# Decode attention in an adaLN block: values in 16384-byte runs, probabilities turned on VectorE, and a loop whose order is written out

## The chip, the cores and the metric

The kernel runs on one core of one Trainium2 chip. Its time is device microseconds for one execution. The engines are PE (TensorE, matrix products), PEld (its weight loads), DVE (VectorE), ACT (ScalarE), POOL (GpSimd) and SP (SyncE, which here only issues transfers). Sixteen DMA engines move data from the memory (HBM) to the on-chip buffers (SBUF); products are written to PSUM.

## What is computed

One decode step of a transformer block for two sequences (B = 2) of one token each, all in float32. The part that matters is the attention in the middle, over the last 4096 keys of a cache:

```python
W = min(4096, max(256, Sk // 4))                       # 4096
q = (x @ wq).reshape(B, Sq, Hq, Dh)                    # 32 heads of 128
k = repeat(k_cache[:, :, Sk - W:, :], rep, axis=1)     # 8 key heads, 4 query heads on each
v = repeat(v_cache[:, :, Sk - W:, :], rep, axis=1)
scores = einsum("bhqd,bhkd->bhqk", q, k) * (Dh ** -0.5)
p = softmax(scores, axis=-1)
o = einsum("bhqk,bhkd->bhqd", p, v)
...                                                    # @ wo, residual, layer norm, SiLU feed-forward
```

Ahead of it stand a modulation (silu(c) @ w_mod), a layer norm and the query product; behind it the product with wo, a second layer norm and a feed-forward with w1 and w2.

## The kernel before

**Transfers.** All loads are issued by SP, in the order of the program: w_mod (4 pieces), wq (4), then for the 16 pairs (h, b) of key head and sequence one key tile and one value tile of 2048 KB, then wo (4), w1 (3) and w2 (5). They share a ring of 8 buffers (`ring`, tag "st", 16 KB on each partition), so a load waits until the buffer eight loads earlier has been read. `load_k` (L77) gives each partition 32 keys in a row, 16384 bytes in one run. `load_v` (L84) gives each partition four runs of 8 values, 4096 bytes each. A small load fills `x_sp` with x (L112), ahead of wq.

**The queries.** The four pieces of wq are multiplied as they land (L263), turned (L272) and spread over a mask `qbd` (L286), so that one product treats the 4 query heads of a key head in 32 columns.

**The loop** (L351) makes 17 steps; step t does the scores and the softmax of pair t and the value products of pair t-1:

- `keys` (L339): DVE turns a key tile in four pieces of 1024 columns, by blocks of 32x32 (L343), into `kT`. The pieces of pair t+1 are placed inside step t (L388, L389, L415, L416).
- PE: scores s, 16 products of 256 columns (L361), four at a time in four column groups. A float32 product is two instructions in the trace, so there are 32.
- DVE: maximum `mx` of each row (L369); PE turns it into one row, `mT` (L371); DVE takes the maximum over the groups, `mg` (L377), and writes it out as `mrow` (L383); PE makes a column of it, `bp` (L391); ACT copies it as `bias` (L393) and does the Exp with sums, `pr` (L395).
- PE turns `pr` by two products with the identity, `pT` (L408), and ACT copies that to `ptb` (L411).
- `weighted` (L296): 32 value products of 128 columns (64 instructions, L305) of the pair before, in two halves that stand on both sides of the softmax; ACT copies the result, `ob` (L314). `collect` (L317) adds it to `o_all` by one product with a selecting matrix `selh` (L319).

The program order is a priority only. A planner of the framework lays each engine's instructions in an order of its own, by what its model takes to be ready. So the value products fill gaps of PE, and things that stand behind the loop in the program (the turns `gaT`, `sbT`, `cbT` and `xT`, L420) run early.

**Behind the loop.** `on` (L452) divides by the sums, four products with `quad` (L455) turn the result, `oTn` (L458) is the operand of wo. 24 products of 512 columns (`acc_o`, L480) and 32 of 128 (`ao`, L489) follow, with a regrouping (`gather`, L462) between; then the second norm and the feed-forward (`hid` L521, `acc_yw` L554, `acc_y` L564), and the output (L577). `xT` is read at L502, `x_sp` at L536.

## Time and profile before

| | us |
|---|---|
| median of 3 runs (lowest to highest) | 241.84 (241.79 to 242.92) |
| the profiled execution itself | 242.15 |
| its span, first to last instruction | 240.0 |
| PE busy in the span | 153.6 |
| DVE busy | 102.5 |
| ACT busy | 34.9 |
| data moved | 97.82 MB, 408 GB/s over the span |
| mean granted clock of PE | 0.844 |

In the profile a line of a group names the line of the kernel, the engine and operation, output and inputs by the program's names, shapes and count; then busy time and mean duration of one in ns; then the idle time of the engine just before these instructions and what ended it. A line of the timeline begins with start and duration in us. A line of a stage begins with its start and end and its length in us, then gives busy time and number of instructions of PE, PEld, DVE, ACT and POOL, then the granted clock of PE (1.00 is full), the busy share of the DMA engines and GB/s. Products are pipelined, so a busy PE isn't a PE at its peak. SPq is SP's queue of transfers.

### The profile page before, as it was taken

The page shows a single profiled execution, that of the slowest core. Times are in us where ns is not written, and L with a number is a line of the kernel's source. Part 1 is how long each engine was busy: PE and PEld are TensorE (multiplying, and loading weights), DVE is VectorE, ACT ScalarE, POOL GpSimd, SP SyncE. Part 2 cuts the span into 40 slices and gives each one's busy share as a digit, 9 for nine tenths or more (in the row PEclk, how much of TensorE's full clock was granted, in tenths as well). Part 3 has the DMA queues.
Part 4 walks back from the last instruction along what each step waited for, and adds up shares of the span by engine and source line. Part 5 has one row for each costly group of instructions (what it writes and reads, how often), then busy time and mean ns, then how long its engine had stood idle before and what let it go on. Part 6 is the DMA issues. An engine that isn't in the chain of part 4 may idle for free.

```text
span 240.0 us, 4597 instructions
## 1 busy us (share of the span) xinstructions
PE 153.6 (64%) x2040; PEld 84.4 (35%) x2040; DVE 102.5 (43%) x179; ACT 34.9 (15%) x96; POOL 7.4 (3%) x27
## 2 busy tenths in 40 slices
PE   0293727345876596386755958478595698936854
PEld 0221101122553373253433625244363466105312
DVE  0604001684656845618548263572745721000230
ACT  2300000101411210202202022020220202020200
POOL 8000000100000000000000000000000000000000
PEclk9999775757999979959979788797978979797779
DMA  6999999999999999999999999999999999999970
GB/s 242 429 434 429 437 426 426 419 440 406 444 417 412 436 412 438 427 411 439 404 440 426 410 438 417 427 426 418 438 414 423 416 436 431 431 430 414 426 309 3
DMA packets 13755, 97.82 MB, mean 408 GB/s; under 512 B 920, under 2 KB 936, under 8 KB 9768
## 3 DMA queue, kind: packets, MB, share of 16 engines
q1 hardware_dynamic: 13736, 97.54, 97.0%
q8 instruction: 16, 0.26, 0.4%
q14 instruction: 3, 0.02, 0.0%
HBM read 97.53 MB, written 0.00 MB: 406 GB/s over the span
## 4 chain that ended last, share of the span: by engine, by line
DMA 65%; PE 17%; DVE 15%; SPq 1%; issue 1%; ACT 0%; DVEq 0%
DMA k<-in_A_k_cache_dram 38%; DMA wo<-in_A_wo_dram 12%; DMA wq<-in_A_wq_dram 12%; DVE kT L343 11%; PE s L361 7%; DMA c_ch<-in_c_dram 2%; PE hid L521 2%; PE o L305 2%; PE q L263 2%; PE acc_yw L554 1%; PE ao L489 1%; PE acc_y L564 1%; SPq L74 1%; PE mT L371 1%; DVE qbd L286 0%
## 5 line engine op out<-in xcount | busy, mean ns | idle before, releaser
L343 DVE STREAM_TRANSPOSE kT<-k 128x1024 f32<-128x1024 f32 x64 | 74.0, 1209 | 6.4 <-DMA k<-in_A_k_cache_dram 6.3
L361 PE MATMUL s<-kT,qbd 128*32 128x256 f32 x512 | 46.8, 519 | 46.6 <-DVE kT L343 46.6
L305 PE MATMUL o<-v,ptb 128*32 128x128 f32 x1024 | 45.8, 300 | 0.0
L361 PEld LDWEIGHTS s<-kT,qbd 128*32 128x32 f32 x512 | 19.4, 140 | 66.0 <-DVE kT L343 50.9
L305 PEld LDWEIGHTS o<-v,ptb 128*32 128x32 f32 x1024 | 37.0, 121 | 5.9 <-issue 3.9
L369 DVE TENSOR_REDUCE mx<-s 128x1 f32<-128x256 f32 x16 | 6.8, 424 | 46.7 <-PE s L361 46.7
L393 ACT COPY bias<-bp 128x1 f32<-128x1 f32 x16 | 2.6, 160 | 120.3 <-PE bp L391 120.3
L263 PE MATMUL q<-wq,hq_T 128*32 128x512 f32 x64 | 12.8, 940 | 10.2 <-DMA wq<-in_A_wq_dram 10.2
L395 ACT ACTIVATE pr<-s,bias 128x256 f32<-128x256 f32 x16 | 11.8, 739 | 0.5
L272 DVE STREAM_TRANSPOSE qT<-q 128x512 f32<-128x512 f32 x2 | 1.4, 716 | 20.1 <-PE q L263 20.1
L263 PEld LDWEIGHTS q<-wq,hq_T 128*32 128x32 f32 x64 | 2.3, 146 | 19.8 <-DMA wq<-in_A_wq_dram 11.0
L480 PE MATMUL acc_o<-wo,oTn 128*32 128x512 f32 x48 | 7.0, 723 | 3.3 <-DMA wo<-in_A_wo_dram 2.9
L377 DVE TENSOR_REDUCE mg<-mT 1x4 f32<-1x64 f32 x16 | 3.3, 209 | 10.9 <-PE mT L371 10.9
L371 PE MATMUL mT<-ident,mx 128*1 128x128 f32 x32 | 7.1, 308 | 1.1 <-DVE mx L369 1.1
L499 DVE STREAM_TRANSPOSE aoT<-ao 128x128 f32<-128x128 f32 x1 | 0.3, 317 | 16.7 <-PE ao L489 16.7
L408 PE MATMUL pT<-ident,pr 128*128 128x128 f32 x32 | 7.0, 301 | 0.4
L391 PEld LDWEIGHTS bp<-negscale,mrow 1*128 1x128 f32 x32 | 4.9, 190 | 5.7 <-DVE mrow L383 4.9
L391 PE MATMUL bp<-negscale,mrow 1*128 1x1 f32 x32 | 6.2, 262 | 0.8 <-DVE mrow L383 0.2
L319 PE MATMUL o_all<-ob,selh 128*32 128x128 f32 x32 | 6.5, 284 | 0.4 <-ACT ob L314 0.4
L411 ACT COPY ptb<-pT 128x256 f32<-128x256 f32 x16 | 6.0, 372 | 4.6 <-PE pT L408 4.5
L195 PE MATMUL mean_a<-mv_a,avg 128*128 128x1 f32 x2 | 0.6, 364 | 8.9 <-DVE mv_a L192 8.9
L227 PE MATMUL m_sp<-wm,scT 128*32 128x512 f32 x32 | 5.7, 796 | 0.0
(123 smaller groups left out, 90.0 us busy)
## 6 DMA issues: line engine op xcount, KB each, us to landing
k<-in_A_k_cache_dram SPq DMA_DIRECT2D x16, 2048.0 KB, 31.5
v<-in_A_v_cache_dram SPq DMA_DIRECT2D x16, 2048.0 KB, 27.0
wq<-in_A_wq_dram SPq DMA_DIRECT2D x4, 2048.0 KB
wo<-in_A_wo_dram SPq DMA_DIRECT2D x4, 2048.0 KB, 27.1
wm<-in_w_mod_dram SPq DMA_DIRECT2D x4, 1536.0 KB, 10.5
w<-in_B_w_dram SPq DMA_DIRECT2D x2, 1024.0 KB, 22.8
w<-in_B_w_dram SPq DMA_DIRECT2D x1, 1792.0 KB
w<-in_B_w_dram SPq DMA_DIRECT2D x2, 896.0 KB
```

The source lines that it names most:

```text
L263: nc.tensor.matmul(q_ps[n][32 * g : 32 * g + 32, :], hq_T[:, k, :], wv[:, n, g], start=(k == 0), stop=(k == 3),)
L305: nc.tensor.matmul(o_ps[32 * i : 32 * i + 32, :], pt[:, n % 2, o : o + 32], vt[:, i, n, :], start=(n == 0), stop=(n == 7),)
L319: nc.tensor.matmul(o_all[:, b, :], selh[:, HQ - G - G * h : 2 * HQ - G - G * h], weighted.o_sb, start=(t == 0), stop=(t == NP - 1), skip_g ...
L343: nc.vector.transpose(kT[t][:, n4].rearrange("p n j r -> p (n j r)"), kt[t][:, n4 * 1024 : (n4 + 1) * 1024],)
L361: nc.tensor.matmul(s_ps[32 * cc : 32 * cc + 32, :], qbd[h // 4][:, h % 4, b, j, :], kT[t][:, :, 2 * cc : 2 * cc + 2, j, :], start=(j == 0) ...
L369: nc.vector.tensor_reduce(mx, s_ps, axis=AX.X, op=ALU.max)
L371: nc.tensor.matmul(mT[0:1, :P], mx, ident, start=True, stop=True)
L391: nc.tensor.matmul(bp[:, 0:1], m, negscale, start=True, stop=True)
L395: nc.scalar.activation(pr.rearrange("p s k n -> p n s k"), s_ps.rearrange("p (n s k) -> p n s k", n=4, s=2), AF.Exp, bias=bias, scale=SCAL ...
L408: nc.tensor.transpose(tp[:, s * P : (s + 1) * P], pr[:, s].rearrange("p k n -> p (k n)"), ident)
L411: nc.scalar.copy(ptb[t % 2][:, :, :P], tp[:, : 2 * P].rearrange("p (s m) -> p s m", s=2))
L480: nc.tensor.matmul(acc[32 * g : 32 * g + 32, :], oTn[:, q, :], wot[q // 8][:, q % 8, :], start=(q < 4), stop=(q >= 20),)
```

## The change

- `load_v` reads values as keys are read: 32 in a row for each partition, one run of 16384 bytes.
- That fixes another order of the probabilities. DVE turns `pr` by 32x32 blocks into `xp` and multiplies it with a mask `group` of the four row groups, spreading it over `zp`; four products with `id4` on PE (`tp`, 128 columns each) sum and permute it; ACT copies 128 columns to `ptb`.
- `weighted` makes 8 products of 512 columns in place of 32 of 128. Its result has 512 columns, of which each row group holds its own block, so `collect` makes four products in place of one, `selh`, `o_all`, `lp`, `on` and `quad` have 128 rows in place of 32, and `lp` takes eight products in place of two.
- Each instruction of the loop is marked to be kept in program order on its engine (`inorder`). Step t now does the turn of pair t's keys and its scores, and in between softmax, turn and value products of pair t-1. The order is: keys 0; mT, mg, mrow; keys 1; bp, bias, Exp, xp, zp; keys 2 and 3; tp, ptb, value products; scores, mx; collect.
- `kT` is laid out by 32-column blocks first, so that a score product reads one stretch of 256 columns.
- The load of `x_sp` stands behind the loads of wo, its turn `xT` behind that. `pr`, `xp`, `zp` and `ob` have one buffer each; `ob` shares one with `qT` and the copies of `gather`.

```diff
--- before.py
+++ after.py
@@ -82,11 +82,11 @@
         return t
 
     def load_v(b, h):
-        t = stream(f"v{h}_{b}").rearrange("p (i m) -> p i m", i=4)
+        t = stream(f"v{h}_{b}")
         nc.sync.dma_start(
-            t, v_cache[b, h, SK - W :, :].rearrange("(i p n) d -> p i (n d)", i=4, p=P)
-        )
-        return t.rearrange("p i (n d) -> p i n d", d=DH)
+            t, v_cache[b, h, SK - W :, :].rearrange("(p n) d -> p (n d)", p=P)
+        )
+        return t
 
...
@@ -109,7 +109,6 @@
                 src[b, :].rearrange("(k a c) -> a k c", k=4, a=4),
             )
     wm += [load_rows("wm", w_mod, k, 6 * D) for k in range(1, 4)]
-    nc.sync.dma_start(rows8(x_sp), x2.rearrange("b (g m) -> g b m", m=P))
     wqt = [load_rows("wq", wq, k, HQ * DH) for k in range(4)]
...
-    selh = const([P, 2 * HQ - G], "selh")
+    group = const([P, 4], "group")
+    nc.vector.tensor_reduce(
+        group, ident.rearrange("p (a r) -> p a r", r=32), axis=AX.X, op=ALU.add
+    )
...
+    selh = const([P, 4, 2 * HQ - G], "selh")
     nc.gpsimd.memset(selh, 0.0)
-    nc.vector.tensor_copy(selh[:, HQ - G : HQ], id4[:, 0:G])
-
-    quad = const([HQ, 4, P], "quad")
+    nc.vector.tensor_copy(
+        selh[:, :, HQ - G : HQ], id4[:, 0:16].rearrange("p (m g) -> p m g", g=G)
+    )
+
+    quad = const([P, 4, P], "quad")
     nc.gpsimd.memset(quad, 0.0)
-    nc.gpsimd.affine_select(
-        out=quad,
-        in_=quad,
-        compare_op=ALU.not_equal,
-        fill=1.0,
-        base=0,
-        pattern=[[-1, 4], [1, P]],
-        channel_multiplier=-4,
-    )
+    for m in range(4):
+        nc.gpsimd.affine_select(
+            out=quad,
+            in_=quad,
+            compare_op=ALU.not_equal,
+            fill=1.0,
+            base=128 * m,
+            pattern=[[-1, 4], [1, P]],
+            channel_multiplier=-4,
+        )
...
-    ptb = [const([P, 2, 160], f"ptb{i}") for i in range(2)]
+    ptb = [const([P, P + 16], f"ptb{i}") for i in range(2)]
...
-        qT = once.tile([P, 4, 4, 32], F32, tag="qT", name=f"qT{n}")
+        qT = once.tile([P, D], F32, tag="wide", name=f"qT{n}").rearrange("p (s j r) -> p s j r", s=4, r=32)
...
-    o_all = bank("O", "o_all")[:HQ, : B * DH].rearrange("p (b d) -> p b d", b=B)
-
-    def weighted(t, b, h, vt, part):
+    o_all = bank("O", "o_all")[:, : B * DH].rearrange("p (b d) -> p b d", b=B)
+
+    def weighted(t, b, h, vt):
+
 
         pt = ptb[t % 2]
-        if part == 0:
-            weighted.o_ps = bank("D", f"o{t}")[:, :DH]
-        o_ps = weighted.o_ps
-        for n in range(4 * part, 4 * part + 4):
-            for i in range(4):
-                o = 32 * (n // 2) + 4 * i
-                nc.tensor.matmul(
-                    o_ps[32 * i : 32 * i + 32, :],
-                    pt[:, n % 2, o : o + 32],
-                    vt[:, i, n, :],
-                    start=(n == 0),
-                    stop=(n == 7),
-                )
-        if part == 1:
-            o_sb = work.tile([P, DH], F32, tag="o_sb", name=f"ob{t}")
-            nc.scalar.copy(o_sb, o_ps)
-            weighted.o_sb = o_sb
-
-    def collect(t, b, h, vt):
-
-        nc.tensor.matmul(
-            o_all[:, b, :],
-            selh[:, HQ - G - G * h : 2 * HQ - G - G * h],
-            weighted.o_sb,
-            start=(t == 0),
-            stop=(t == NP - 1),
-            skip_group_check=True,
-        )
+        o_ps = bank("D", f"o{t}")
+        for n in range(8):
+            c = n % 4
+            inorder(nc.tensor.matmul(
+                o_ps[32 * c : 32 * c + 32, :],
+                pt[:, 16 * n : 16 * n + 32],
+                vt[:, 512 * n : 512 * n + 512],
+                start=(n < 4),
+                stop=(n >= 4),
+            ))
+        o_sb = once.tile([P, 4 * DH], F32, tag="wide", name=f"ob{t}")
+        inorder(nc.scalar.copy(o_sb, o_ps))
+        return o_sb
+
+    def collect(t, b, h, o_sb):
+
+        for m in range(4):
+            inorder(nc.tensor.matmul(
+                o_all[32 * m : 32 * m + 32, b, :],
+                selh[:, m, HQ - G - G * h : 2 * HQ - G - G * h],
+                o_sb[:, m * DH : (m + 1) * DH],
+                start=(t == 0),
+                stop=(t == NP - 1),
+                skip_group_check=True,
+            ))
...
     def keys(t, n4):
 
         if n4 == 0:
-            kT[t] = ktp.tile([P, 4, 8, 4, 32], F32, tag="kT", name=f"kT{t}")
-        nc.vector.transpose(
-            kT[t][:, n4].rearrange("p n j r -> p (n j r)"),
-            kt[t][:, n4 * 1024 : (n4 + 1) * 1024],
-        )
-
+            kT[t] = ktp.tile([P, 4, 32, 32], F32, tag="kT", name=f"kT{t}")
+        inorder(nc.vector.transpose(
+            kT[t][:, :, 8 * n4 : 8 * n4 + 8, :].rearrange("p j n k -> p n j k"),
+            kt[t][:, n4 * 1024 : (n4 + 1) * 1024].rearrange("p (n j r) -> p n j r", j=4, r=32),
+        ))
+
...
+    inorder = tc.keep_in_program_order
     fetch(0)
-    for n4 in range(4):
-        keys(0, n4)
+    s_ps, mx = {}, {}
     for t in range(NP + 1):
-        prev = None
-        if t > 0:
-            prev = (t - 1, seq[t - 1][1], seq[t - 1][0], vt[t - 1])
-        if t < NP:
-            h, b = seq[t]
+        last, now = t > 0, t < NP
+        if now:
             fetch(t + 1)
-            s_ps = bank("A", f"s{t}")[:, :256]
-            for j in range(4):
-                for cc in range(4):
-                    nc.tensor.matmul(
-                        s_ps[32 * cc : 32 * cc + 32, :],
-                        qbd[h // 4][:, h % 4, b, j, :],
-                        kT[t][:, :, 2 * cc : 2 * cc + 2, j, :],
-                        start=(j == 0),
-                        stop=(j == 3),
-                    )
-            mx = work.tile([P, 1], F32, tag="mx", name=f"mx{t}")
-            nc.vector.tensor_reduce(mx, s_ps, axis=AX.X, op=ALU.max)
-            mT = bank("B", f"mT{t}")
-            nc.tensor.matmul(mT[0:1, :P], mx, ident, start=True, stop=True)
-        if prev:
-            weighted(*prev, 0)
-        if t < NP:
-            m = mrow[t % 2]
-            mg = work.tile([1, G], F32, tag="mg", name=f"mg{t}")
-            nc.vector.tensor_reduce(
+            keys(t, 0)
+        if last:
+            u = t - 1
+            h, b = seq[u]
+            mT = bank("B", f"mT{u}")
+            inorder(nc.tensor.matmul(mT[0:1, :P], mx[u], ident, start=True, stop=True))
+            m = mrow[u % 2]
+            mg = work.tile([1, G], F32, tag="mg", name=f"mg{u}")
+            inorder(nc.vector.tensor_reduce(
                 mg,
                 mT[0:1, :P].rearrange("o (c i g) -> o g c i", c=4, g=G)[:, :, :, 0:4],
                 axis=AX.XY,
                 op=ALU.max,
-            )
-            nc.vector.tensor_copy(
+            ))
+            inorder(nc.vector.tensor_copy(
                 m.rearrange("o (c i g) -> o c i g", c=4, g=G)[:, :, 0:4, :],
                 mg[:, None, None, :].to_broadcast([1, 4, 4, G]),
-            )
-            if t + 1 < NP:
-                keys(t + 1, 0)
-                keys(t + 1, 1)
-            bp = bank("B", f"bp{t}")
-            nc.tensor.matmul(bp[:, 0:1], m, negscale, start=True, stop=True)
-            bias = work.tile([P, 1], F32, tag="bias", name=f"bias{t}")
-            nc.scalar.copy(bias, bp[:, 0:1])
-            pr = work.tile([P, 2, 32, 4], F32, tag="pr", name=f"pr{t}")
-            nc.scalar.activation(
-                pr.rearrange("p s k n -> p n s k"),
-                s_ps.rearrange("p (n s k) -> p n s k", n=4, s=2),
+            ))
+        if now:
+            keys(t, 1)
+        if last:
+            bp = bank("B", f"bp{u}")
+            inorder(nc.tensor.matmul(bp[:, 0:1], m, negscale, start=True, stop=True))
+            bias = work.tile([P, 1], F32, tag="bias", name=f"bias{u}")
+            inorder(nc.scalar.copy(bias, bp[:, 0:1]))
+            pr = once.tile([P, 8, 32], F32, tag="pr", name=f"pr{u}")
+            inorder(nc.scalar.activation(
+                pr.rearrange("p s k -> p (s k)"),
+                s_ps[u],
                 AF.Exp,
                 bias=bias,
                 scale=SCALE,
                 accum_out=rowsum[:, h, b : b + 1],
-            )
-        if prev:
-            weighted(*prev, 1)
-        if t < NP:
-            tp = bank("C", f"pT{t}")
-            for s in range(2):
-                nc.tensor.transpose(
-                    tp[:, s * P : (s + 1) * P], pr[:, s].rearrange("p k n -> p (k n)"), ident
-                )
-            nc.scalar.copy(
-                ptb[t % 2][:, :, :P], tp[:, : 2 * P].rearrange("p (s m) -> p s m", s=2)
-            )
-            if t + 1 < NP:
-                keys(t + 1, 2)
-                keys(t + 1, 3)
-        if prev:
-            collect(*prev)
-
-    gaT, sbT, cbT, xT = turned(ga, "gaT"), turned(sb, "sbT"), turned(cb1, "cbT"), turned(x_sp, "xT")
+            ))
+
+            xp = once.tile([P, 8, 32], F32, tag="xp", name=f"xp{u}")
+            inorder(nc.vector.transpose(xp, pr))
+            zp = once.tile([P, 4, 8, 16], F32, tag="zp", name=f"zp{u}")
+            inorder(nc.vector.tensor_mul(
+                zp,
+                xp[:, None, :, 0:16].to_broadcast([P, 4, 8, 16]),
+                group[:, :, None, None].to_broadcast([P, 4, 8, 16]),
+            ))
+        if now:
+            keys(t, 2)
+            keys(t, 3)
+        if last:
+            tp = bank("C", f"pT{u}")[:, :P]
+            for i in range(4):
+                inorder(nc.tensor.matmul(
+                    tp[32 * i : 32 * i + 32, :],
+                    id4,
+                    zp.rearrange("p c s x -> p (c s) x")[:, :, 4 * i : 4 * i + 4],
+                    start=True,
+                    stop=True,
+                ))
+            inorder(nc.scalar.copy(ptb[u % 2][:, :P], tp))
+            o_sb = weighted(u, b, h, vt[u])
+        if now:
+            s_ps[t] = bank("A", f"s{t}")[:, :256]
+            for j in range(4):
+                for cc in range(4):
+                    inorder(nc.tensor.matmul(
+                        s_ps[t][32 * cc : 32 * cc + 32, :],
+                        qbd[seq[t][0] // 4][:, seq[t][0] % 4, seq[t][1], j, :],
+                        kT[t][:, j, 8 * cc : 8 * cc + 8, :],
+                        start=(j == 0),
+                        stop=(j == 3),
+                    ))
+            mx[t] = work.tile([P, 1], F32, tag="mx", name=f"mx{t}")
+            inorder(nc.vector.tensor_reduce(mx[t], s_ps[t], axis=AX.X, op=ALU.max))
+        if last:
+            collect(u, b, h, o_sb)
+
+    gaT, sbT, cbT = turned(ga, "gaT"), turned(sb, "sbT"), turned(cb1, "cbT")
...
     for q0 in range(0, 32, 8):
         wot.append(load_runs("wo", wo, 32, q0, q0 + 8))
+    nc.sync.dma_start(rows8(x_sp), x2.rearrange("b (g m) -> g b m", m=P))
+    xT = turned(x_sp, "xT")
...
     for b in range(B):
-        nc.tensor.matmul(
-            lp[:HQ, b : b + 1], rx[:, b].rearrange("p h g -> p (h g)"), ones, start=True, stop=True
-        )
-    rl = once.tile([HQ, B], F32, tag="rl", name="rl")
-    nc.vector.reciprocal(rl, lp[:HQ, :B])
-    on = once.tile([HQ, B, DH], F32, tag="on", name="on")
+        for m in range(4):
+            nc.tensor.matmul(
+                lp[32 * m : 32 * m + 32, b : b + 1],
+                rx[:, b].rearrange("p h g -> p (h g)"),
+                ones,
+                start=True,
+                stop=True,
+            )
+    rl = once.tile([P, B], F32, tag="rl", name="rl")
+    nc.vector.reciprocal(rl, lp[:, :B])
+    on = once.tile([P, B, DH], F32, tag="on", name="on")
```

2 lines of the change are left out of this document (1 added, 1 removed).

## The prediction

> **What bounds the kernel now.** I read the page's chain of work first, then the DMA share by stage, then the clock.
>
> ```profile
> span 240.0 us, 4597 instructions
> ...
> DMA 65%; PE 17%; DVE 15%; SPq 1%; issue 1%; ACT 0%; DVEq 0%
> ```
>
> ```profile
> 64.00:180.00 116.00, 81.41 (x1304) 51.76 (x1296) 65.86 (x86) 19.45 (x64) 0.00 (x0) 0.87 1.02 424
> 196.00:214.00 18.00, 13.54 (x180) 6.72 (x173) 1.64 (x7) 1.80 (x6) 0.00 (x0) 0.87 1.02 433
> ```
>
> The end hangs on transfers, and the DMA engines never rest: share 1.02 in the loop (64 to 180 us, keys and values mixed, 424 GB/s) and behind it (196 to 214, wo in 16384-byte runs, 433). One step of the loop needs one key and one value tile, 2 x 2.097 MB, so DMA allows a step every 4.194/0.424 = **9.89 us**. The loop must only stay below that.
>
> **Part 1, the transfers.** Values now come in 4096-byte runs and would come in 16384-byte runs. The mixed stage runs at 424, the unmixed one at 433. If the whole loop ran at 433, a step would take 9.69 us, so 16 steps gain 16 x 0.20 = 3.2 us; the lower bound is nothing (part of the difference may come from tensors and not runs). This counts only while DMA sets the pace.
>
> **Part 2, the length of a loop step.** Before, value products fill PE while DVE turns the next keys. After, PE's order is fixed: mT, bp, tp, value products o(u), scores s(t), collect. So o(u) waits for the whole softmax and the turn of the same step, s(t) is queued behind o(u), the maximum mx(t) behind s(t), and on DVE the first key turn of the next step behind mx(t), even if its keys landed long ago. I count from the start of mx(u) on DVE. Prices:
>
> ```profile
> L343 DVE STREAM_TRANSPOSE kT<-k 128x1024 f32<-128x1024 f32 x64 | 74.0, 1209 | 6.4 <-DMA k<-in_A_k_cache_dram 6.3
> ...
> L213 DVE STREAM_TRANSPOSE cT<-c_ch 128x128 f32<-128x128 f32 x1 | 0.3, 311 | 5.7 <-DMA c_ch<-in_c_dram 5.7
> ...
> L238 DVE TENSOR_TENSOR h_a<-xn_a,mod_ch 128x128 f32<-128x128 f32 x1 | 0.3, 293 | 0.0
> ```
>
> ```profile
> 54.45 0.42 DVE L369 TENSOR_REDUCE mx<-s 128x1 f32<-128x256 f32 x1 [1.20 <-PE s L361]
> 54.79 1.24 DVE L343 STREAM_TRANSPOSE kT<-k 128x1024 f32<-128x1024 f32 x1
> 55.95 0.17 DVE L377 TENSOR_REDUCE mg<-mT 1x4 f32<-1x64 f32 x1
> ```
>
> ```profile
> 67.65 1.94 PE L361 MATMUL s<-kT,qbd 128*32 128x256 f32 x32 [1.48 <-DVE kT L343]
> ...
> 69.65 0.42 DVE L369 TENSOR_REDUCE mx<-s 128x1 f32<-128x256 f32 x1 [2.06 <-PE s L361]
> ...
> 70.55 0.21 DVE L377 TENSOR_REDUCE mg<-mT 1x4 f32<-1x64 f32 x1 [0.47 <-PE mT L371]
> 70.79 0.18 DVE L383 COPY mrow<-mg 1x64 f32<-1x64 f32 x1
> ...
> 72.43 0.44 PE L408 MATMUL pT<-ident,pr 128*128 128x128 f32 x2
> ...
> 72.91 0.37 ACT L411 COPY ptb<-pT 128x256 f32<-128x256 f32 x1 [0.19 <-PE pT L408]
> ```
>
> ```profile
> 199.71 1.95 PE L305 MATMUL o<-v,ptb 128*32 128x128 f32 x64
> ...
> 204.73 1.93 PE L480 MATMUL acc_o<-wo,oTn 128*32 128x512 f32 x8 [0.36 <-DVE oTn L458]
> ```
>
> At full clock a step then goes:
> - mx, one key turn, mg: mg starts at 1.50 (54.45 to 55.95, the same order as in the change); mrow 0.24 later, at 1.74.
> - bp, bias and Exp: from mrow to the first reader of the probabilities 72.43 - 70.79 = 1.64, so 3.38. The second key turn (1.85 to 3.0) lies beside it.
> - xp, a turn of 256 columns: not in the trace. 128 columns take 0.31 and 1024 take 1.21, so 0.001 per column: 0.44 as an estimate, bounds 0.31 and half of 1.21. zp, a product of 512 columns: 0.29 for 128 and 0.001 a column more, 0.68 as an estimate, bounds 0.29 and 1.21. Both are in series: 3.38 + 0.47 + 0.69 + 0.05 to reach PE = 4.59 for tp.
> - tp (8 instructions of 128 columns for pT's 2), then the ptb copy 0.48 later (72.43 to 72.91) and the first product 0.42 after that (copy 0.37 and a handover): 5.5. tp's operand is read in pieces of 16 bytes, which no row shows: bounds 0.2 less and, by the acc_o row below, 0.5 more (8 instructions of 512 columns take 0.97 at full clock, pT 0.44).
> - o(u): 16 instructions of 512 columns. The acc_o row has 8 of them in 1.93 us at clock 0.50 (its window stands in part 3), so 16 take 3.86 there and 1.93 at 1.00, as much as the 64 of today (1.95, at 1.00): PE gains nothing from the wider form. End 7.43. The key turns 3 and 4 are over at 3.38 + 1.11 + 2 x 1.16 = 6.8 and don't decide.
> - s(t): 67.65 to the next mx 2.00, so the step is **9.43 us**, below 9.89.
>
> **Part 3, the clock.** The granted clock changes only at the edges of a grid of 3.41 us; these rows are windows of that grid (first column of figures: length, PE busy; PEclk third from the end):
>
> ```profile
> 64.15:67.56 3.41, 2.01 (x52) 1.30 (x40) 3.41 (x4) 0.98 (x4) 0.00 (x0) 1.00 0.95 400
> 67.56:70.98 3.42, 3.33 (x70) 2.20 (x70) 0.86 (x5) 0.00 (x0) 0.00 (x0) 1.00 1.03 420
> 101.70:105.11 3.41, 2.49 (x24) 1.19 (x28) 0.86 (x1) 0.00 (x0) 0.00 (x0) 0.50 1.04 443
> 105.11:108.53 3.42, 3.42 (x50) 2.40 (x42) 0.94 (x4) 0.00 (x0) 0.00 (x0) 0.50 0.93 382
> 122.18:125.59 3.41, 3.11 (x32) 1.50 (x36) 0.25 (x1) 0.00 (x0) 0.00 (x0) 0.50 0.98 420
> 125.59:129.01 3.42, 3.34 (x78) 2.48 (x70) 2.24 (x5) 1.10 (x4) 0.00 (x0) 1.00 0.99 409
> 129.01:132.42 3.41, 0.70 (x8) 0.29 (x10) 3.19 (x3) 0.43 (x2) 0.00 (x0) 1.00 1.09 448
> 132.42:135.83 3.41, 3.41 (x40) 1.76 (x36) 0.00 (x0) 0.00 (x0) 0.00 (x0) 0.50 0.98 418
> 190.45:193.86 3.41, 1.27 (x24) 0.81 (x28) 2.08 (x2) 0.00 (x0) 0.00 (x0) 1.00 1.02 414
> 193.86:197.27 3.41, 3.41 (x53) 2.53 (x42) 0.82 (x3) 0.00 (x0) 0.00 (x0) 0.50 1.07 448
> 197.27:200.69 3.42, 3.40 (x76) 2.54 (x78) 0.38 (x2) 1.53 (x5) 0.00 (x0) 1.00 1.04 444
> 204.10:207.51 3.41, 3.05 (x18) 0.68 (x17) 0.27 (x1) 0.00 (x0) 0.00 (x0) 0.50 1.01 432
> ```
>
> A window with 0.70 or 1.27 us of PE work is followed by one at 0.50, a window with 2.01 is not. A window at 0.50 ends the slow spell if it holds 3.11 us of work, not if it holds 2.49. After the change PE has, between about 0.9 (mT done) and 5.5 (o starts), only bp and tp, some 0.8 us. Any window that starts between -0.1 and 2.9 holds 1.27 us or less: 3.0 of 3.41 us of phases, so practically each step has a poor window and a half-clock one behind it, which falls on o and s. Let it start at h, from mx:
> - h = 5.5: 3.35 us of work in it, so one slow window; it does 1.68 of o and s (3.87 in all); the rest at full clock ends at 11.0. Step 11.1. The next step's h is 5.5 - 11.1 + three windows (10.24) = 4.6.
> - h = 4.6: tp is 0.2 slower, o starts at 5.7; 2.9 us of work, between 2.49 and 3.11, taken as enough. Half clock until 8.0 does 1.15; end 10.7, step 10.8, next h = 4.05.
> - h = 4.05: work 0.6 + 1.8 = 2.4, not enough, a second slow window up to 10.9: o ends at 9.6, s does 0.65 by then, the rest ends at 12.2. Step 12.2, next h 5.5.
>
> The cycle closes: 11.1 + 10.8 + 12.2 = 34.1 us, ten windows, **11.37 us a step**. DMA is then late no more: its share in the loop falls to about 9.7/11.4 = 0.85, key and value buffers come free later, and part 1 is worth nothing.
>
> **Part 4, the ends.** Step 0 is as before: mx(0) at 54.45 (row above). mx(15) = 54.45 + 15 x 11.37 = 225.0. The last step has no key turns: mg at 0.90 (70.55 - 69.65), products from 4.9, o ends at 6.8 to 8.8 by clock, say 7.8. From o's end to acc_o today 204.73 - 201.66 = 3.07; the copy is four times as wide (by ptb's 0.37 for 256 columns some 0.35 more as an estimate), so 3.4: acc_o starts at 236.2. Today it then waits for wo; now all of wo is there.
>
> ```profile
> 219.70 1.70 PE ao L489 x32
> ```
>
> This is ao's last part today, done at 221.40. After, acc_o's 48 instructions take 5.8 at full clock (8 in 1.93 at half), ao's 64 take 1.95 (like o's 64), its gather 0.4; a half window at the start costs 1.7: 9.85, so ao is done at 246.0. From ao to the end of the span it is 18.6 us today; the w1 and w2 buffers free up by then (the last, 256 KB, needs wo's last buffer and some 3 us, and is read over 10 us later). Span 264.6. The profiled execution took 242.15 for a span of 240.0, 2.15 more; the median 241.84 is 0.3 lower. So **266 us**.
>
> Costed at nothing: the larger constants (three more selects and bigger fills on POOL, which nobody needs before the queries), lp's six extra products and the wider `on` (beside other work of the last step). Without that cover the selects would cost 3 x 0.7 us by zp's estimate, the others a few tenths.
>
> **The rivals.**
> 1. *Not slower.* bp, mT and tp count as activity that keeps the clock up. Each single gap of PE is at most 2.2 us (from bp, which ends near 2.4, to tp). Or the planner doesn't keep the order and fills the gap with products as today. Then a step is 9.43 or less and DMA sets the pace at 9.69: 241.84 - 3.2 = 239 us, down to no gain. The Trainium skill, page "TensorE: Matmul & The Clock Gate", section "HAM oscillation", gives this rule: no idle gap of PE over about 3.4 us. By that rule alone the clock would stay up here; the trace disagrees, since 129.01 to 132.42 holds 0.70 us of work, its idle stretch is under 2.8 us, and 0.50 follows. What counts by the rows is a window's share. Chance 0.13, and 0.03 for a gain too small to see (within 0.5%, about what a measurement can tell).
> 2. *Three windows.* If xp, zp and tp are at their lower bounds, a step may lock to three windows, 10.24: 15 x 1.13 = 17 less, 249 us. Chance 0.08.
> 3. *The moved load.*
>
> ```profile
> 17.92 0.40 DVE L248 STREAM_TRANSPOSE xT<-x_sp 128x128 f32<-128x128 f32 x1 [5.87 <-DMA x_sp<-in_A_x_dram]
> ```
>
> Today xT sits in DVE's queue ahead of h_a. If it stays there while its load moves behind wq on SP, DVE is blocked until wq has landed; the q products (8 instructions of 512 columns in 1.93 at half clock, 64 in 7.7 at full and about 9.4 with a slow start) then come in one lump, some 5 us later: 271 us. Chance 0.08. Otherwise the load, one small issue on SP behind wo's, and its turn are hidden under the loop.
>
> **How the numbers follow.** Forecast 0.68. Its bounds: xp, zp and tp together 0.7 less or 1.2 more a step; less saves at most 0.7 (10.7, the shortest step of the cycle), 15 x 0.7 = 10; more takes 15 x 1.2 = 18: 256 to 284. The range reaches down to rival 2: 249 to 284, leaving out rival 1. Faster 0.13, same 0.03, slower 0.84.
>
> **What would show it.** Right: in the loop four of ten grid windows at 0.50, starts of mx 10.7 to 12.3 apart, DVE waiting for s before mx 3 us and more a step, SP waiting on key turns and value products, DMA share near 0.85, ao long after wo. Wrong: PEclk 1.00 through the loop, or mx under 10 us apart with DVE waiting for keys. Wrong in size: xp over 0.6, zp over 0.9 or tp to ptb over 0.7.

## The result and the profile after

The changed kernel takes 253.97 us in the median of 4 runs (252.45 to 254.68), the kernel before 242.31 beside it (241.79 to 242.92, 4 runs): ratio 1.0472, 95% interval 1.0412 to 1.0532. It is 11.7 us slower. The forecast was 24 us slower, so the direction was right and the size more than twice too large. 253.97 lies within the stated range of 249 to 284, but only because that range was stretched down to rival 2; the forecast's own bounds, 256 to 284, missed it.

The page of the changed kernel (its profiled execution took 254.44 us):

```profile
span 252.7 us, 3508 instructions
...
PEclk9997597675978979779575977978879786657979
...
PE 49%; DVE 23%; DMA 15%; ACT 8%; issue 4%; SPq 0%; DVEq 0%; ACTq 0%
...
L349 DVE STREAM_TRANSPOSE kT<-k 128x1024 f32<-128x1024 f32 x64 | 77.0, 1224 | 0.0
...
L433 DVE TENSOR_REDUCE mx<-s 128x1 f32<-128x256 f32 x16 | 6.8, 425 | 62.8 <-PE s L425 62.8
...
L401 DVE TENSOR_TENSOR zp<-xp,group 128x512 f32<-128x512 f32 x16 | 11.1, 692 | 0.5
...
L399 DVE STREAM_TRANSPOSE xp<-pr 128x256 f32<-128x256 f32 x16 | 7.1, 445 | 4.3 <-ACT pr L389 2.9
...
L389 ACT ACTIVATE pr<-s,bias 128x256 f32<-128x256 f32 x16 | 7.6, 474 | 0.7 <-ACT bias L387 0.2
```

The chain that ended last was 65% transfers; it is now 49% PE, 23% DVE and 15% transfers. The key turns waited 6.3 us for keys before and wait 0.0 now; DVE stands 62.8 us before `mx`, waiting for scores, where it stood 46.7 before. The clock row never stays at 9 in the loop: each dip is half-clock time.

Where the 12.7 us between the two spans lie is read from the first and the last `mx` of each timeline. Changed kernel:

```profile
53.48 0.42 DVE L433 TENSOR_REDUCE mx<-s 128x1 f32<-128x256 f32 x1 [2.87 <-PE s L425]
...
213.78 0.42 DVE L433 TENSOR_REDUCE mx<-s 128x1 f32<-128x256 f32 x1 [5.34 <-PE s L425]
```

Kernel before (its first stands at 54.45):

```profile
195.09 0.42 DVE L369 TENSOR_REDUCE mx<-s 128x1 f32<-128x256 f32 x1 [2.55 <-PE s L361]
...
212.68 1.92 PE L480 MATMUL acc_o<-wo,oTn 128*32 128x512 f32 x16 [2.92 <-DMA wo<-in_A_wo_dram]
...
217.51 1.76 PE L489 MATMUL ao<-wo,oTn 128*32 128x128 f32 x32 [2.91 <-DMA wo<-in_A_wo_dram]
```

The start is 1.0 us earlier (in the profiles of all runs here the first `mx` stands between 51.6 and 54.5, so this need not be the change's doing). The fifteen steps between take 160.3 us for 140.6 (19.7 more: 10.69 a step for 9.38), and from the last `mx` to the end it is 38.9 us for 44.9 (6.0 less; the products with wo, which stood twice for 2.9 us waiting for it, find it landed). 19.7 - 6.0 - 1.0 = 12.7. The whole loss is in the loop. Starts of `mx` apart, in us, from the timelines of all kernels whose steps matter below:

```
changed             11.68 10.32 10.28 10.26 10.25 10.24 11.94 11.10 10.65 10.40 10.39 10.31 10.28 10.26 11.94
e1 (filled)         10.18  8.90  8.90  8.90  8.90  8.90  8.90  9.27  9.80  9.65  9.77  9.68 10.47 11.48  8.90
e3 (0.2 us later)   13.01 10.88 10.62 10.49 12.06 11.16 10.62 10.51 12.07 11.16 10.62 10.52 12.07 11.16 10.62
e5 (order alone)    10.50  9.59  9.65  7.97  9.64  9.65  7.97  9.74  9.93  9.79 11.02 10.12  9.82  9.79 10.52
e6 (strided Exp)    13.50 11.24 10.75 12.18 11.23 10.73 12.18 11.22 10.83 12.13 11.03 10.74 12.25 11.26 10.74
e9 (0.27 shorter)   12.83 10.90 10.42 10.38 10.31 10.27 10.26 10.25 10.35 10.19 10.22 10.23 10.23 10.24 10.24
e10 (0.40 shorter)  11.77 10.25 10.24 10.24 10.24 10.24 10.24 10.24 10.33 10.19 10.22 10.23 10.24 10.24 10.24
```

The changed kernel settles towards 10.24, which is three windows of the clock's grid (in the rows below, 107.06 to 127.54 is six windows, 20.48 us, so one is 3.413), slips once to 11.94, settles again and slips again. One settled step in the timeline:

```profile
106.27 0.42 DVE L433 TENSOR_REDUCE mx<-s 128x1 f32<-128x256 f32 x1 [3.66 <-PE s L425]
...
108.81 0.47 ACT L389 ACTIVATE pr<-s,bias 128x256 f32<-128x256 f32 x1
...
109.41 0.45 DVE L399 STREAM_TRANSPOSE xp<-pr 128x256 f32<-128x256 f32 x1
109.89 0.69 DVE L401 TENSOR_TENSOR zp<-xp,group 128x512 f32<-128x512 f32 x1
...
110.73 0.65 PE L412 MATMUL pT<-zp,id 128*32 128x128 f32 x8 [2.14 <-DVE zp L401]
...
111.75 2.96 PE L311 MATMUL o<-v,ptb 128*32 128x512 f32 x16 [0.38 <-ACT ptb L419]
...
114.53 1.90 PE L425 MATMUL s<-kT,qbd 128*32 128x256 f32 x32
...
116.51 0.42 DVE L433 TENSOR_REDUCE mx<-s 128x1 f32<-128x256 f32 x1 [3.65 <-PE s L425]
```

And windows of the clock's grid, the columns as in the prediction:

```profile
107.06:110.48 3.42, 0.45 (x3) 0.29 (x2) 3.25 (x6) 0.72 (x3) 0.00 (x0) 1.00 0.98 422
110.48:113.89 3.41, 2.79 (x20) 0.83 (x24) 2.38 (x3) 0.27 (x1) 0.00 (x0) 0.50 1.01 432
...
120.72:124.13 3.41, 2.78 (x20) 0.82 (x24) 2.39 (x3) 0.27 (x1) 0.00 (x0) 0.50 1.05 452
124.13:127.54 3.41, 3.41 (x28) 1.16 (x24) 0.00 (x0) 0.59 (x1) 0.00 (x0) 0.50 0.98 413
```

The window 107.06 to 110.48 holds 0.45 us of PE work, because DVE and ACT work on the probabilities; the next runs at 0.50 and falls on tp and the value products, which take 2.96 us for 1.92 at full clock (e1 below). With 2.79 us of work that window ends the slow spell. One step later the same window holds 2.78, and a second slow one follows: that is the step of 11.94.

Transfers by stage:

```profile
64.00:180.00 116.00, 72.53 (x753) 26.96 (x748) 70.61 (x99) 17.27 (x56) 0.00 (x0) 0.81 1.01 430
...
210.00:240.00 30.00, 23.53 (x252) 9.74 (x248) 4.92 (x21) 4.17 (x9) 0.00 (x0) 0.72 0.74 283
```

In the loop DMA stays as busy as before (share 1.01, now 430 GB/s for 424), and the granted clock is 0.81 for 0.87. DMA rests only behind the loop: from 220 to 230 us its share is 0.62 and then 0.30, where the kernel before had 1.00 and 1.01.

### The profile page after: what moved, and what is told of

It reads as the page before. It is cut to its first block, busy times and chain, and to the rows that moved or that the text cites. A ratio compares the mean times of both kernels' runs of the same rounds, so it can differ in the third digit from the quotient of the medians.

```text
span 252.7 us, 3508 instructions
## 1 busy us (share of the span) xinstructions
PE 153.7 (61%) x1476; PEld 55.6 (22%) x1476; DVE 119.3 (47%) x212; ACT 35.5 (14%) x96; POOL 9.3 (4%) x30
## 4 chain that ended last, share of the span: by engine, by line
PE 49%; DVE 23%; DMA 15%; ACT 8%; issue 4%; SPq 0%; DVEq 0%; ACTq 0%
PE o L311 20%; PE s L425 13%; DMA wq<-in_A_wq_dram 12%; DVE kT L349 9%; DVE zp L401 4%; PE pT L412 4%; ACT pr L389 4%; DVE xp L399 3%; PE acc_o L504 3%; DVE mx L433 3%; DMA wm<-in_w_mod_dram 2%; PE bp L385 2%; ACT ptb L419 2%; PE q L271 1%; PE acc_yw L578 1%
## 5 line engine op out<-in xcount | busy, mean ns | idle before, releaser
L311 PE MATMUL o<-v,ptb 128*32 128x512 f32 x256 | 51.3, 945 | 6.0 <-ACT ptb L419 6.0
L425 PE MATMUL s<-kT,qbd 128*32 128x256 f32 x512 | 36.8, 411 | 2.5 <-DVE kT L349 2.3
L433 DVE TENSOR_REDUCE mx<-s 128x1 f32<-128x256 f32 x16 | 6.8, 425 | 62.8 <-PE s L425 62.8
L412 PE MATMUL pT<-zp,id 128*32 128x128 f32 x128 | 10.1, 403 | 33.8 <-DVE zp L401 33.6
L311 PEld LDWEIGHTS o<-v,ptb 128*32 128x32 f32 x256 | 9.5, 158 | 34.0 <-issue 21.0
L319 ACT COPY ob<-o 128x512 f32<-128x512 f32 x16 | 9.4, 587 | 53.4 <-PE o L311 53.4
L401 DVE TENSOR_TENSOR zp<-xp,group 128x512 f32<-128x512 f32 x16 | 11.1, 692 | 0.5
L412 PEld LDWEIGHTS pT<-zp,id 128*32 128x32 f32 x128 | 3.6, 135 | 34.7 <-issue 34.5
L399 DVE STREAM_TRANSPOSE xp<-pr 128x256 f32<-128x256 f32 x16 | 7.1, 445 | 4.3 <-ACT pr L389 2.9
L419 ACT COPY ptb<-pT 128x128 f32<-128x128 f32 x16 | 4.3, 266 | 32.5 <-PE pT L412 32.5
L389 ACT ACTIVATE pr<-s,bias 128x256 f32<-128x256 f32 x16 | 7.6, 474 | 0.7 <-ACT bias L387 0.2
```

The costliest lines, as they stand in the source:

```text
L311: inorder(nc.tensor.matmul(o_ps[32 * c : 32 * c + 32, :], pt[:, 16 * n : 16 * n + 32], vt[:, 512 * n : 512 * n + 512], start=(n < 4), stop ...
L319: inorder(nc.scalar.copy(o_sb, o_ps))
L389: inorder(nc.scalar.activation(pr.rearrange("p s k -> p (s k)"), s_ps[u], AF.Exp, bias=bias, scale=SCALE, accum_out=rowsum[:, h, b : b + 1],))
L399: inorder(nc.vector.transpose(xp, pr))
L401: inorder(nc.vector.tensor_mul(zp, xp[:, None, :, 0:16].to_broadcast([P, 4, 8, 16]), group[:, :, None, None].to_broadcast([P, 4, 8, 16]),))
L412: inorder(nc.tensor.matmul(tp[32 * i : 32 * i + 32, :], id4, zp.rearrange("p c s x -> p (c s) x")[:, :, 4 * i : 4 * i + 4], start=True, st ...
```

## The experiments

My theory: the two things of the change that touch PE together, the order (value products behind the softmax) and the longer way of the probabilities (xp, zp, tp), leave PE a poor stretch in each step; a half-clock window follows and falls on the value products; the step, 8.90 us at full clock, then no longer fits under DMA's 9.75 (4.194/0.430). Rivals: the chain of dependent work alone is too long; VectorE's added work (1.14 us a step) is the bound; the order alone costs it; the runs of 16384 bytes do harm. Ratios below are to the kernel before on the same chip.

### e1: unread products that fill PE's poor stretch

```diff
+            warm(tpf, 1)
             inorder(nc.tensor.matmul(bp[:, 0:1], m, negscale, start=True, stop=True))
+            warm(tpf, 2)
...
+    def warm(bank_, n):
+        for _ in range(n):
+            inorder(nc.tensor.matmul(bank_[:, P:], ident, idle, start=True, stop=True))
```

One product stands behind mT, two behind bp. `idle` is 384 columns of `qbd[0]`, and nobody reads the results.

> The changed kernel with three products more in each loop step, whose result nobody reads: one of 384 columns behind mT and two behind bp, where PE has next to nothing to do. Nothing else moves. Clock theory (the step is long because a poor window of 3.41 us is followed by one at half clock that falls on value products and scores): the granted clock stays at 1.00 in the loop, a step falls from 10.69 to the 9.75 us that DMA allows at 430 GB/s, and the time to 239 to 242 us. Chain rival (the step is long because the value products stand in the chain between softmax and scores, the clock matters little): 250 us or more. VectorE rival (the turn xp and the product zp make DVE the bound): no change, 254.

239.17 us (238.27 to 239.87), ratio 0.9922 (0.9896 to 0.9947). Its chain:

```profile
DMA 56%; PE 19%; DVE 17%; ACT 4%; issue 2%; SPq 1%; POOL 0%; ACTq 0%; POOLq 0%
```

Its stage row and one step:

```profile
64.00:180.00 116.00, 93.02 (x904) 42.65 (x903) 81.43 (x115) 19.73 (x64) 0.00 (x0) 0.99 1.01 430
```

```profile
80.81 0.42 DVE L442 TENSOR_REDUCE mx<-s 128x1 f32<-128x256 f32 x1 [2.30 <-PE s L434]
...
83.36 0.47 ACT L398 ACTIVATE pr<-s,bias 128x256 f32<-128x256 f32 x1
...
83.96 0.45 DVE L408 STREAM_TRANSPOSE xp<-pr 128x256 f32<-128x256 f32 x1
...
85.18 0.42 PE L421 MATMUL pT<-zp,id 128*32 128x128 f32 x8 [0.56 <-DVE zp L410]
...
86.00 1.92 PE L311 MATMUL o<-v,ptb 128*32 128x512 f32 x16 [0.39 <-ACT ptb L428]
...
87.73 1.91 PE L434 MATMUL s<-kT,qbd 128*32 128x256 f32 x32
...
89.71 0.42 DVE L442 TENSOR_REDUCE mx<-s 128x1 f32<-128x256 f32 x1 [2.30 <-PE s L434]
```

More work on PE makes the kernel faster than the changed one, by some 13 us (the two ratios, 1.0472 - 0.9922, of 242). The clock stays at 0.99, every dependent instruction is still there, and a step is 8.90 until DMA's pace takes over (9.65 to 9.8, but for two steps, 10.47 and 11.48, in each of which one window ran at half clock). The chain is long enough to matter only at half clock, and VectorE isn't the bound: both of those rivals fall. The Trainium skill, page "TensorE: Matmul & The Clock Gate", section "HAM oscillation", asks only that PE has no idle gap over about 3.4 us. The changed kernel's longest in the step shown is 2.14 us, ahead of tp, and its clock still falls; by the trace the rule isn't strict enough.

### e2: value products one step later, as filling

```diff
-    for t in range(NP + 1):
+    for t in range(NP + 2):
...
+            weighted(w, vt[w], o_ps, 0)
...
+            weighted(w, vt[w], o_ps, 1)
```

Four products of pair t-2 stand behind mT, four behind bp.

> The changed kernel with the value products one step later: in step t PE does those of pair t-2, four products behind mT and four behind bp, so they are out of the chain and fill PE's gap with work that is needed. The values stay in the ring one step longer. Clock theory: few or no half-clock windows before the scores; the chain without value products is about 8.6 us, so DMA sets the pace at 9.75: 238 to 242 us. Chain rival: the same. VectorE rival: xp and zp are still there and the time stays near 254.

239.01 us (238.08 to 240.18), ratio 0.9927 (0.9900 to 0.9953). Steps are 8.60 at full clock and 9.7 at DMA's pace, with one of 11.84. The clock is 0.93 in the loop, not 0.99: some half-clock windows are left, but the time is the same as with unread products. This version and e1 are both faster than either kernel, by 0.7 to 0.8% of the time before. With DMA at 430 GB/s and a share of 1.01 there, I expect no more from the loop; no run tried it.

### e3: the softmax 0.2 us later

```diff
-            inorder(nc.scalar.copy(bias, bp[:, 0:1]))
+            inorder(nc.scalar.copy(bias0, bp[:, 0:1]))
+            inorder(nc.scalar.copy(bias, bias0))
```

> The changed kernel with one more small copy on ACT between bp and Exp (bias is copied twice), 0.2 us more in the chain of each step, as if Exp took 0.67 in place of 0.47 us. Clock theory: the slow window begins earlier against the products, the step loses its hold on three windows (10.24 us) and goes through the forecast's cycle of steps with one and with two slow windows, about 11.4 in the mean: 254 + 15 x 0.7 = 264 us. Chain rival (each step simply is as long as its chain): 15 x 0.2 = 3 more, 257. VectorE rival: no change, 254.

260.2 us (258.57 to 261.31), ratio 1.0797 (1.0758 to 1.0835), some 8 us over the changed kernel by the ratios; the clock theory had said 10, a fixed price per step 3. The steps fall into a cycle of four (11.16, 10.62, 10.51, 12.07; 44.36 us, 13 windows). 0.2 us a step costs 0.48 (11.17 for 10.69). A window that shows how:

```profile
100.92:104.33 3.41, 2.56 (x20) 0.82 (x24) 2.61 (x3) 0.27 (x1) 0.00 (x0) 0.50 1.01 432
```

The value products come 0.2 us later into it, it holds 2.56 us of work instead of 2.79, and a second slow window follows. That happens once in every cycle.

### e4: only the 16384-byte runs

```diff
-            t, v_cache[b, h, SK - W :, :].rearrange("(i p n) d -> p i (n d)", i=4, p=P)
+            t, v_cache[b, h, SK - W :, :].rearrange("(p n) d -> p (n d)", p=P)
```

> The kernel before with one edit: values are read in runs of 16384 bytes. The products then take values in another order than the probabilities, so the output is not the reference's; all work is as before. If the runs are what made the loop's transfers faster (424 GB/s before, 430 after the change) and DMA sets the pace of the kernel before: 16 x 0.14 to 0.20 = 2 to 3 us less, 239 to 240. Rival (the steps of the kernel before are set by its own half-clock windows, and DMA is waited for in a few steps only): within 0.5% of 242.3.

239.95 us (238.66 to 240.92), ratio 0.9955 (0.9931 to 0.9979): 1.1 us less, not 2 to 3. That is a gain of 0.45%, so the rival (within 0.5%) came nearer than my own expectation.

```profile
64.00:180.00 116.00, 82.08 (x1316) 52.93 (x1308) 67.53 (x87) 19.99 (x65) 0.00 (x0) 0.87 1.01 429
```

The runs do no harm; they lift the loop from 424 to 429 GB/s. They bring less than 16 x 0.12 us = 1.9; the likely reason, argued and not tried apart, is that some steps (8.5 to 11 us) wait for PE, not for transfers.

### e5: only the order

The kernel before, with old values, `pr`, `pT` and 128-column value products, in the changed kernel's written-out order:

```diff
-                nc.tensor.matmul(
+                inorder(nc.tensor.matmul(
                     o_ps[32 * i : 32 * i + 32, :],
                     pt[:, n % 2, o : o + 32],
                     vt[:, i, n, :],
                     start=(n == 0),
                     stop=(n == 7),
-                )
+                ))
```

> The kernel before with the loop order of the change and nothing else of it: values in 4096-byte runs, pT by two products with the identity, 32 value products of 128 columns, all pinned in the order keys 0, mT, keys 1, bp, Exp, keys 2 and 3, pT, ptb, value products, scores, mx, collect. Clock theory: the chain at full clock is about 8.0 us (no xp and zp, Exp 0.74), PE's poor stretch is 3.4 us and not 4.5, so a poor window comes in some steps only, and DMA at 9.89 us a step covers a slow window when there is one: 241 to 248 us. Order rival (the order by itself costs what the change costs): 252 to 256 us.

240.65 us (240.38 to 242.55), ratio 1.0003 (0.9975 to 1.0032): the order alone costs nothing, so the order rival falls. Yet its clock falls too:

```profile
64.00:180.00 116.00, 77.63 (x1250) 57.44 (x1250) 64.31 (x86) 18.19 (x60) 0.00 (x0) 0.85 1.02 424
```

```profile
73.24 0.42 DVE L411 TENSOR_REDUCE mx<-s 128x1 f32<-128x256 f32 x1 [4.30 <-PE s L403]
...
77.47 3.14 PE L303 MATMUL o<-v,ptb 128*32 128x128 f32 x64 [0.46 <-ACT ptb L395]
...
82.88 0.42 DVE L411 TENSOR_REDUCE mx<-s 128x1 f32<-128x256 f32 x1 [4.35 <-PE s L403]
...
90.86 0.43 DVE L411 TENSOR_REDUCE mx<-s 128x1 f32<-128x256 f32 x1 [2.68 <-PE s L403]
```

A step is 7.97 us at full clock (82.88 to 90.86) and 9.64 with one half-clock window in it (73.24 to 82.88). 9.64 still lies under DMA's 9.89, so the window is free. The changed kernel's chain is 0.93 us longer; with the same window, which costs up to 1.7 us, it is over 10. The layout alone isn't the loss either: e1 and e2 have all of it and take 239 us. That is the change's loss in one line: **not the order and not the layout, but the layout's longer chain in that order**.

### e6: Exp writes with a stride, as before

```diff
-            pr = once.tile([P, 8, 32], F32, tag="pr", name=f"pr{u}")
+            pr = once.tile([P, 32, 8], F32, tag="pr", name=f"pr{u}").rearrange("p k s -> p s k")
```

> The changed kernel with Exp writing its output in steps of 32 bytes (and xp reading it so), as the kernel before writes it in steps, so that Exp should take the 0.74 us that the forecast put in. Clock theory: the forecast's cycle comes back, 11.2 to 11.4 us a step: 262 to 265 us. Chain rival: 16 x 0.27 = 4 more than the changed kernel, 258.

262.79 us (262.21 to 266.08), ratio 1.0944 (1.0871 to 1.1017).

```profile
L399 DVE STREAM_TRANSPOSE xp<-pr 128x256 f32<-128x256 f32 x16 | 10.1, 634 | 6.9 <-ACT pr L389 6.9
...
L389 ACT ACTIVATE pr<-s,bias 128x256 f32<-128x256 f32 x16 | 11.5, 718 | 0.7 <-ACT bias L387 0.2
```

```profile
88.90 0.42 DVE L433 TENSOR_REDUCE mx<-s 128x1 f32<-128x256 f32 x1 [3.80 <-PE s L425]
...
123.04 0.42 DVE L433 TENSOR_REDUCE mx<-s 128x1 f32<-128x256 f32 x1 [3.79 <-PE s L425]
```

Exp takes 0.72 us again, and xp, which now reads with that stride, 0.63 for 0.45. The value products start 0.36 us later behind `mx` than in the changed kernel (5.84 for 5.48), so a step is some 9.26 at full clock. And the forecast's cycle is there: 12.18, 11.23, 10.73, ten windows (88.90 to 123.04 is 34.14), where the forecast had 12.2, 11.1, 10.8 and 34.1. The chain rival, 258, falls. The Trainium skill, page "SBUF — State Buffer", section "Door 1: The DMA port swizzle", says that consecutive accesses to the same line of 16 bytes run at full rate and that each step to a new line costs something. These two rows agree: at a step of 32 bytes, where every element has a line of its own, both take longer (0.72 for 0.47 us, 0.63 for 0.45). The section gives no price, but by it the row of the strided Exp was no price for the contiguous one.

### e7: no written-out order

```diff
-    inorder = tc.keep_in_program_order
+    inorder = lambda instruction: instruction
```

> The changed kernel without the marks that keep program order, so that the planner orders each engine. It puts the scores ahead of the value products, with mT behind these. Clock theory: products and scores still stand together and mT, bp and tp alone in between, so the poor stretch is as long as before (about 5 us) and nearly each step has a half-clock window: 248 to 260 us. Order rival (the pinned order is the cost, the planner would do better): 240 to 243.

294.25 us (one execution 288.4, the other three 293.69 to 294.89; too far apart for a ratio). The profile is that of the one of 294.81. Both expectations missed, by far. The planner puts the scores ahead of the value products, as I thought, but all four key turns behind zp:

```profile
121.81 4.62 DVE L349 STREAM_TRANSPOSE kT<-k 128x1024 f32<-128x1024 f32 x4
```

The scores then wait for keys, and nearly all steps stand at 13.5 to 13.65, four windows, two of them at half clock. So the planner's order is worse for this layout than the written-out one; even the execution of 288.4 is over 30 us behind the changed kernel. How the loss divides between the key turns and the clock I didn't separate.

### e8: filling with thin products

```diff
-            inorder(nc.tensor.matmul(bank_[:, P:], ident, idle, start=True, stop=True))
+            inorder(nc.tensor.matmul(bank_[:, P:], idle[0:1, :P], idle[0:1, :], start=True, stop=True))
```

> The three added products of the first experiment with one row of the array in place of 128 (same columns, same time on PE), result unread. If the granted clock follows the share of a window in which PE is busy: as with 128 rows, clock 1.00 in the loop and 239 us. If it follows how much of the array works: as without them, half-clock windows in each step and 252 to 256 us. The window from 200.69 in the kernel before (2.24 us busy, much of it in thin products, followed by 0.50) speaks for the second.

251.22 us (248.89 to 252.18), ratio 1.0449 (1.0403 to 1.0494): as slow as the change.

```profile
115.15:118.56 3.41, 2.61 (x8) 1.10 (x8) 3.24 (x7) 0.72 (x3) 0.00 (x0) 1.00 0.98 413
118.56:121.97 3.41, 2.93 (x20) 0.80 (x24) 2.32 (x3) 0.27 (x1) 0.00 (x0) 0.50 1.02 437
```

The filled window shows 2.61 us of PE work, more than the 2.01 that kept the clock up in the kernel before, and still half clock follows. e1's products have the same duration (535 ns each, here 525) and 128 rows instead of one. So busy time is not what is counted; it matters how much of the array works. The weights changed with it (the identity in e1, a row of `qbd` here), so a part of the values in this wasn't tried apart, and how the count goes between one row and 128 wasn't measured. The run also shows that the added instructions as such are not what helped in e1.

### e9 and e10: a shorter chain

```diff
-                zp,
-                xp[:, None, :, 0:16].to_broadcast([P, 4, 8, 16]),
+                zp[:, :2],
+                xp[:, None, :, 0:16].to_broadcast([P, 2, 8, 16]),
```

This is e9; e10 has 1 for 2.

> The changed kernel with zp formed for two of the four row groups only (256 columns; the other half of zp is zero from the start, so that half of the probabilities is left out of the result). By the rows of zp (0.69 us for 512 columns) and of a 128-column product (0.29) it takes 0.43, so the chain of a step is 0.27 shorter: 8.63 us at full clock where the warmed run had 8.90. Clock theory (a half-clock window costs half of the PE work that it covers, so a step of 8.63 to 8.90 can settle at exactly three grid windows; the window starts later behind mx, near 4.4, holds over 3 us of PE work and always ends): all steps 10.24 to 10.35, none of 11 or more once it has settled, so 15 x (10.69 - 10.28) = 6 us less than the changed kernel, 247 to 249. Rival, each step pays its chain and a fixed loss: 15 x 0.27 = 4 us less, 250, with steps of 10.0 and, now and then, 11.7. Rival, DMA or VectorE: no change, 254.

> As the run before, with zp formed for one row group only (128 columns, 0.29 us): the chain is 0.40 shorter than in the changed kernel, 8.50 us at full clock. Clock theory: one window can cost at most half of 3.41, 1.7 us, so a step is at most 10.2 and cannot hold three windows; the phase drifts slowly, nearly all steps at 10.1 to 10.2 for as long as it takes the window to slide past the scores, then some shorter: 244 to 247. Rival, chain and fixed loss: 15 x 0.40 = 6 us less than the changed kernel, 248. Rival, DMA or VectorE: no change, 254.

e9: 247.03 us (245.36 to 249.05), ratio 1.0208 (1.0149 to 1.0268). e10: 245.61 us (243.81 to 248.79), ratio 1.0148 (1.0062 to 1.0234). Both medians lie in the clock theory's bounds; by the ratios, e9's rival (250) falls, and e10's (248) can't be told apart by time. The profiled execution was the longest of the four in both (249.05 and 248.79), so what follows is shown for it alone: in the shortest, 245.36 and 243.81, some steps must have been shorter. e9's steps do what the theory said: 10.19 to 10.42 from the third on, no slip. Of e10 I had said that it couldn't hold three windows; in this execution it does, to the last hundredth:

```profile
106.85 0.42 DVE L434 TENSOR_REDUCE mx<-s 128x1 f32<-128x256 f32 x1 [4.04 <-PE s L426]
...
117.09 0.42 DVE L434 TENSOR_REDUCE mx<-s 128x1 f32<-128x256 f32 x1 [4.04 <-PE s L426]
```

```profile
111.67:115.08 3.41, 3.37 (x16) 0.79 (x20) 1.37 (x2) 0.00 (x0) 0.00 (x0) 0.50 1.01 432
```

With 3.37 us of work the slow window costs about what is missing, 10.24 - 8.50 = 1.74. Either the most that it can cost, 1.7, was put 0.04 too low, or the chain of 8.50, which was worked out and not measured, was. A chain 0.13 us shorter than e9's changes nothing in a settled step: there the clock, not the chain, sets the length. The difference of the two medians can't be told from their spread.

## Why the prediction was right in direction and wrong in size

**What bounded the kernel, and part 1 (transfers): right.** Long runs are faster, 424 to 430 GB/s in the loop, and bring little (e4, 1.1 us within the forecast's nothing to 3.2), and in the changed kernel no gain shows, since no key turn waits for its transfer there.

**Part 2 (the full-clock step of 9.43) is the step that failed.** The order of the work, every wait, and the estimates for xp (0.44; measured 0.445) and zp (0.68; 0.692) were right. Three other terms were too large; e1's step above, counted from `mx`, has them:

| start behind mx | forecast | e1 | mis-sized term |
|---|---|---|---|
| xp | 3.38 | 3.15 | Exp, priced by the row before (739 ns, written with a stride), takes 474 ns written in order; 0.22 of the 0.26 shows |
| tp | 4.59 | 4.37 | same 0.22 |
| value products | 5.50 | 5.19 | ptb to the first product: 0.32, not 0.42 |
| next mx | 9.43 | 8.90 | the scores start 1.73 behind the first value product, not 1.93: they overlap its last ones |

0.22 + 0.09 + 0.22 = 0.53 us a step. The chief one I could have seen: the change itself rewrites Exp's output from strided to contiguous, and I carried over a row with another access pattern. None of the three terms had bounds; only xp, zp and tp had. The own lower bound, 256, goes by a shortest step of 10.7, the shortest of the cycle. The measured mean, 10.69, is as short for another reason, the settling at three windows; the start and the end make up the rest.

**Part 3 (the clock): the mechanism was right, the outcome hung on the wrong sum.** Poor window, half-clock window behind it on o and s, enough work in it or a second one: the windows above show each. Worked again with 8.90: let the slow window start 4.36 us behind `mx`. It delays tp and its copy by 0.29 and does half of the work in the 2.29 us of o and s that lie in it (5.48 to 7.77), so 1.14 is lost: 8.90 + 0.29 + 1.14 = 10.33. That is 0.09 over three windows, so the next slow window starts 0.09 earlier, covers 0.09 less, and the step is half of that shorter. The excess over 10.24 should halve each time; measured were 0.08, 0.04, 0.02, 0.01, 0.00. The step rests at three windows. The forecast's longer chain leaves less than 2.79 us of work in that window at 10.24, cannot rest, and slips every third step: 11.37. e6 (some 9.26) does that, e3 (some 9.10) every fourth step, the changed kernel (8.90) twice in the loop, e9 and e10 (8.63, 8.50) never once settled. The mean of 10.69 instead of 11.37, over 15 steps, is 10.2 us of the 12 that the forecast was too long; the rest is the start (1.0) and the end (0.7).

The prediction took "2.9, between 2.49 and 3.11", as enough work for a slow window. In the changed kernel the edge lies at 2.78 to 2.79, so the choice fell right, though no row that it showed decides it. The edge is also why 0.2 us decides so much. It isn't one number for all work: in e4 a half-clock window with 2.67 us (120.85 to 124.27) ended the slow spell, in e7 one with 2.84 us of scores (123.78 to 127.20) did not. That agrees with e8: busy time is not quite what is counted.

**The DMA share of 0.85 was wrong.** In the loop it is 1.01. The step is longer than DMA needs by 10.69 - 9.75 = 0.94 us, 14 us over the loop; the eight buffers hold 8 x 4.88 = 39 us of transfers, so these can run that far ahead (a count, not tried by a run), and DMA rests behind the loop. For the time nothing follows from it.

**Part 4 (the ends): right in the sum, by errors that offset.**

```profile
226.56 0.40 DVE L256 STREAM_TRANSPOSE xT<-x_sp 128x128 f32<-128x128 f32 x1
...
226.74 6.92 PE L504 MATMUL acc_o<-wo,oTn 128*32 128x512 f32 x48 [0.36 <-DVE oTn L482]
...
234.67 1.06 PE L513 MATMUL ao<-wo,oTn 128*32 128x128 f32 x32
```

From the last `mx` to `acc_o` it is 12.96 (forecast 11.2, with o at half clock almost throughout, 3.64), to the end of ao 9.0 more (9.85), to the end of the span 17.0 more (18.6): 38.9 for 39.6, from 1.8 too little and 0.9 and 1.6 too much.

**The rivals.** Rival 1: the clock didn't stay up and the order was kept; refuted, though e1 and e2 show that its time, 239, is what the loop gives with PE kept at work. Rival 2, three windows, is what mostly happened, and its 249 is nearer than the forecast; but it was put down to xp, zp and tp at their lower bounds, and these came at their estimates. It was given 0.08 because its condition was sought in the unknown rows only, not in the rows taken as known. Rival 3: xT waited for nothing (row above); refuted.

## What to carry to other kernels

A half-clock window costs nothing while the step it falls on stays under what the transfers need; so before dependent work moves in series on PE, add one such window (up to 1.7 us here) to the step and compare that with the transfers' pace. Where a step lies between, its length snaps to whole windows, and small terms count several times over or not at all: price each known instruction again if the change alters its access pattern. A shorter chain helped less here (e9 and e10, 6 to 8 us off by the ratios) than work in the poor stretch: three unread products, or the value products of the step before, took some 13 us off.

## What the hardware showed beside that

- Products of one row keep PE busy by the profile (2.61 of 3.41 us) and don't keep its clock; the same number of products of 128 rows does (e8, e1).
- A loop can lock to the clock's grid: steps of 10.24 us with chains of 8.50, 8.63 and 8.90 us (e10, e9, the changed kernel; the first two worked out from zp's rows), of 13.65, four windows, in e7.
- Exp over 256 columns takes 0.474 us written in order and 0.72 to 0.74 with a stride of 16 or 32 bytes; the 32x32 turn of 256 columns 0.445 read in order and 0.634 read with a stride of 32 bytes.
